# Cluster attention and two MoE layers on one core: probabilities times v over three query tiles at a time instead of two

## The chip, the cores and the metric

The kernel runs on one core of one Trainium2 chip. The metric is the device time of one execution in microseconds; the median of three executions counts. One execution was also profiled, and all rows below are from it. PE is the matrix engine, DVE, ACT and POOL are the three engines for elementwise work, and SP issues the DMAs. PE writes its results to PSUM, in banks of 512 fp32 per partition.

## The reference

```python
q_assign = argmax(q_n @ c_n)      # nearest of 16 centroids, per head; k_assign the same
mask = q_assign[..., :, None] == k_assign[..., None, :]
scores = where(mask, q @ k.T / sqrt(64), -1e9)
attn = exp(scores - max(scores)); attn = attn / (sum(attn) + 1e-9)
x = attn @ v                      # batch 2, 8 heads, 768 tokens, 64 per head -> x [1536, 512]
h = x @ w_in                      # [1536, 1024]
solu = h * softmax(h); ln = layernorm(solu) * g_ln
x = ln @ w_out                    # [1536, 512]
out = ((x @ w_a) * (x @ w_b)) @ w_out2   # inner width 1536
```

Everything is fp32.

## The kernel before

Attention goes over 8 pairs of heads (`n`), two heads `j` in each, six query tiles `t` of 128 rows in each head: 96 steps. A step computes the scores of one query tile against all 768 keys (`score`, PE L989, into one of the two buffers `psS`), their maximum (DVE L993), the exponentials with their sum (ACT L997, into `P_`), and transposes them in two halves of three key tiles (`turn`, PE L1021, into `psT`). The halves are copied to the buffer at `PT_` by DVE (L1028) or ACT (L1030), in turns. `PT_` holds two buffers, one for each group of `GT = 2` query tiles.

After every second step a group is complete, and probabilities times v is run for it (`apply`, PE L1047): six key tiles, each one call to `T.matmul` of 64 columns of v (stationary) against 256 moving columns. Even key tiles go to the left half of the array's columns and so to the upper 64 partitions of `psO`, odd ones to the right half and the lower 64. The six are planned as two pieces (`part` 0 and 1) of three key tiles each, which other PE work may come between. Then ACT copies one half of `psO` (L1061), DVE adds the other (L1062), and, when both heads of the pair are there, the sum of exponentials is inverted (L1067, L1069), spread, transposed (L1077), multiplied in (L1080), and the result is split into a high and a low part for the MoE. In the code there are 8 x 2 x 3 groups, so 96 pieces of three key tiles; the profile has two PE records for each such call.

The two heads of the next pair are prepared between the steps: loads of q, k, v (`do_load`, L658), transposes (`qk_part`, L729), which write the split q and k into a buffer `hl`, similarities to the centroids (`do_sims`: matmul L818, copy to SBUF by ACT L826, transposes L822, reduction L828 into `sim`), the argmax (`do_arg`), one-hots (`ohp`, transposes in `do_oh` and, for the first pair, `do_oh0` L882), and DMAs that place the parts for the score matmuls (`do_place`, L805; `do_ohd`, L911). `hl` has two buffers, used in turns. `do_sims` copies its matmul's result into the buffer of the one-hots.

The first MoE follows, over 12 tiles of 128 tokens (`moe_h` L1140, layer norm, `moe_lnt` L1213, `moe_x2` L1230), then the second (L1283, L1311). Their weights are loaded and split by DVE, ACT and POOL as they are needed; pieces for the second MoE's weights go to 25 places (`PIECES`), three of which are free before the first MoE ends.

The order of all instructions is made at build time by a planner (`Plan`): each operation has an engine, a cost, a rank and what it reads and writes, and a list scheduler sorts them. `ADJ` is a table of additions to the ranks, and `PVC` is the cost that the planner takes for one piece of probabilities times v. Every engine then runs its list strictly in order.

Of the kernel before, what the change touches and what calls it, by code (L numbers as in the profile page):

```python
# [49 lines left out]
    "centroids 0 DVE": 9.936, "centroids 0 PE": 14.146, "centroids 0 POOL": -10.837,  # L50
    "centroids 0 SP": -527.444, "centroids ACT": -19.438, "centroids DVE": 112.978, "centroids PE": -12.208,
    "centroids POOL": -0.395, "centroids SP": 4.39, "direct 0.0 ACT": -59.405, "direct 0.0 DVE": -104.641,
    "direct 0.0 PE": -57.582, "direct 0.1 ACT": -138.753, "direct 0.1 DVE": 1.547, "direct 0.1 PE": -26.219,
    "direct ACT": 76.379, "direct DVE": 60.391, "direct PE": 32.904, "do_arg 0.0.0 DVE": 3.705,
# [11 lines left out]
    "do_load SP": -224.464, "do_oh 1.0 ACT": 1.581, "do_oh 1.0 PE": -8.205, "do_oh 1.1 ACT": 6.451,  # L66
# [23 lines left out]
    "do_sims 5.0 PE": -1.25, "do_sims 5.1 ACT": 7.966, "do_sims 5.1 DVE": 14.282, "do_sims 5.1 PE": 9.306,  # L90
    "do_sims 6.0 ACT": -22.098, "do_sims 6.0 DVE": 71.424, "do_sims 6.0 PE": -51.606,
    "do_sims 6.1 ACT": 45.722, "do_sims 6.1 DVE": -71.608, "do_sims 6.1 PE": -11.805,
    "do_sims 7.0 ACT": 1.712, "do_sims 7.0 DVE": 43.106, "do_sims 7.0 PE": -6.351, "do_sims 7.1 ACT": 0.278,
    "do_sims 7.1 DVE": 1.564, "do_sims 7.1 PE": 17.891, "do_sims ACT": 13.823, "do_sims DVE": -14.384,
    "do_sims PE": -451.772, "gains 0 DVE": 1.737, "gains 0 PE": -123.102, "gains DVE": 10.842,
# [298 lines left out]
def tile_cluster_attention_moe_moe2(  # L394
# [239 lines left out]
    def hlo(n):  # L634
        return HLS[n % 2]
# [759 lines left out]
```

## Time and profile before

| what | us |
|---|---|
| median of 3 executions (751.42 to 752.21) | 751.48 |
| the profiled execution | 752.12 |
| its span from first to last instruction | 750.30 |

A group of instructions of a page or of a view by line is given as line, engine, operation, output <- input, shape and count, then busy time in us, mean ns of one, and idle time of the engine before them with what ended it. The busy time of PE includes an instruction's way through the array, so two that follow each other overlap in the rows; what an instruction costs PE is read here from start to next start in the timeline.

### The profile page before, as it was taken

How to read it: one execution, taken by the hardware profiler on the slowest of the kernel's cores; microseconds unless marked ns; L12 is line 12 of the kernel's file. 1: busy time of each engine (PE TensorE's matmuls, PEld its weight loads, DVE VectorE, ACT ScalarE, POOL GpSimd, SP SyncE). 2: the span in 40 equal slices, each digit the busy share in tenths (PEclk: the TensorE clock that was granted, in tenths of full speed). 3: DMA queues.
4: the chain of work that ended last, by engine and by line, in shares of the span. 5: the costliest groups of instructions: out<-in, count | busy, mean ns of one | idle time of the engine just before them, and what ended most of it. 6: DMA issues, size and time to landing. Idle time of an engine off the chain costs nothing.

```text
span 750.3 us, 11135 instructions
## 1 busy us (share of the span) xinstructions
PE 735.9 (98%) x4152; PEld 590.3 (79%) x4152; DVE 444.6 (59%) x792; ACT 348.6 (46%) x697; POOL 269.4 (36%) x317
## 2 busy tenths in 40 slices
PE   7899999999999999999999999999999999999997
PEld 6667677677777777788998999888888888888886
DVE  5667775867776787699997926882138211112212
ACT  5666676576667666456535544343144211211110
POOL 2116452346264332457461527872047300000000
PEclk8899999999999999999999999999999999999999
DMA  4168545327265211223140222342011000100101
GB/s 149 47 142 206 138 113 130 89 73 156 81 149 126 62 56 41 80 89 113 57 141 2 85 85 94 104 145 80 1 57 56 1 0 1 57 0 1 57 0 57
DMA packets 39093, 58.49 MB, mean 78 GB/s; under 512 B 3832, under 2 KB 33920, under 8 KB 39040
## 3 DMA queue, kind: packets, MB, share of 16 engines
q1 hardware_dynamic: 39040, 57.79, 26.8%
q8 instruction: 33, 0.54, 0.3%
q14 instruction: 20, 0.16, 0.1%
HBM read 36.74 MB, written 3.15 MB: 53 GB/s over the span
## 4 chain that ended last, share of the span: by engine, by line
PE 89%; DVE 5%; DMA 2%; ACT 1%; POOL 1%; issue 1%; SPq 0%; DVEq 0%; ACTq 0%; POOLq 0%
PE psS L1311 13%; PE psT L1283 13%; PE psO L1047 13%; PE psT L1021 9%; PE psS L989 9%; PE psO L1283 7%; PE psM L1283 7%; PE psS L1140 5%; PE psO L1230 4%; PE psM L1230 4%; PE psM L729 1%; PE psM L818 1%; DMA F<-in_moe_w_in_dram 1%; PE psT L1213 1%; DMA F<-in_moe_w_out_dram 1%; PE psM L901 1%
## 5 line engine op out<-in xcount | busy, mean ns | idle before, releaser
L479 POOL TENSOR_TENSOR R<-F,R 128x512 fp32r<-128x512 f32 (+1 forms) x76 | 89.0, 1176 | 73.3 <-ACT R L605 69.5
L1047 PE MATMUL psO<-F 128*64 128x256 f32 x576 | 104.2, 400 | 1.3 <-DVE F L1062 1.3
L1283 PE MATMUL psT<-R 128*128 128x512 f32 x432 | 103.5, 389 | 0.0
L1311 PE MATMUL psS<-R 128*128 128x512 f32 x432 | 103.5, 389 | 0.0
L993 DVE TENSOR_REDUCE mxn<-psS 128x1 f32<-128x768 f32 x96 | 91.3, 952 | 17.8 <-PE psS L989 16.2
L997 ACT ACTIVATE F<-psS,mxn 128x768 f32<-128x768 f32 x96 | 86.8, 904 | 17.7 <-DVE mxn L993 14.4
L1311 PEld LDWEIGHTS psS<-R 128*128 128x128 f32 x432 | 81.0, 188 | 16.8
L1283 PEld LDWEIGHTS psT<-R 128*128 128x128 f32 x432 | 81.0, 188 | 16.8
L989 PE MATMUL psS<-R 128*128 128x512 f32 (+3 forms) x384 | 92.9, 365 | 0.0
L1021 PE MATMUL psT<-ident,F 128*128 128x128 f32 x576 | 90.4, 278 | 0.9 <-ACT F L997 0.4
L1021 PEld LDWEIGHTS psT<-ident,F 128*128 128x128 f32 x576 | 64.8, 140 | 22.7 <-issue 9.2
L989 PEld LDWEIGHTS psS<-R 128*128 128x128 f32 (+1 forms) x384 | 66.5, 193 | 14.5 <-issue 4.6
L596 POOL TENSOR_TENSOR F<-F 128x512 int32<-128x512 int32 x45 | 62.0, 1381 | 38.1 <-DVE F L592 32.6
L1028 DVE COPY F<-psT 128x384 f32<-128x384 f32 x96 | 53.1, 553 | 34.7 <-PE psT L1021 30.9
L1047 PEld LDWEIGHTS psO<-F 128*64 128x64 f32 x576 | 45.7, 137 | 32.9 <-issue 13.4
L1140 PE MATMUL psS<-R 128*128 128x512 f32 x288 | 69.7, 395 | 0.7 <-DVE F L1161 0.7
L1294 ACT COPY F<-psT 128x512 f32<-128x512 f32 x36 | 21.1, 586 | 97.3 <-PE psT L1283 95.7
L1140 PEld LDWEIGHTS psS<-R 128*128 128x128 f32 x288 | 52.8, 188 | 12.7 <-DVE F L1161 1.2
L1030 ACT COPY F<-psT 128x384 f32<-128x384 f32 x96 | 45.9, 478 | 34.5 <-PE psT L1021 32.9
L1296 ACT CAST R<-F 128x512 fp32r<-128x512 f32 x36 | 22.3, 621 | 81.4 <-DVE F L1295 79.9
L1295 DVE TENSOR_TENSOR F<-psO,F 128x512 f32<-128x512 f32 x18 | 12.4, 691 | 73.5 <-PE psO L1283 73.5
L1295 DVE TENSOR_TENSOR F<-psM,F 128x512 f32<-128x512 f32 x18 | 12.4, 690 | 72.5 <-PE psM L1283 72.5
(148 smaller groups left out, 1101.3 us busy)
## 6 DMA issues: line engine op xcount, KB each, us to landing
F<-in_moe_w_out_dram SPq DMA_DIRECT2D x20, 512.0 KB, 3.2
R<-R SPq DMA_DIRECT2D x28, 288.0 KB, 4.6
F<-in_moe_w_a_dram SPq DMA_DIRECT2D x12, 512.0 KB, 3.5
F<-in_moe_w_b_dram SPq DMA_DIRECT2D x12, 512.0 KB, 3.4
R<-R SPq DMA_DIRECT2D x28, 192.0 KB, 4.8
F<-in_moe_w_in_dram SPq DMA_DIRECT2D x8, 512.0 KB, 4.7
F<-in_v_dram SPq DMA_DIRECT2D x8, 384.0 KB, 4.2
out_dram<-F SPq DMA_DIRECT2D x12, 256.0 KB, 2.1
```

The source lines that it names most:

```text
L479: pl.add("POOL", pool(n), rank, lambda: G.tensor_tensor(out=out_, in0=in0, in1=in1, op=ALU.subtract), reads, writes)
L596: pl.add("POOL", pool(n), rank, lambda: G.tensor_tensor(out=u, in0=u, in1=low, op=ALU.add), [rk, lwk], [uk])
L989: T.matmul(sp[:, c0:c0 + cn], kq[:r, 2 * m, t * P:(t + 1) * P], kq[:r, 2 * m + 1, c0:c0 + cn], start=m == 0, stop=m == 1)
L993: pl.add("DVE", dve(S), i + SUB["max"], lambda: V.tensor_reduce(out=mxn[:, b:b + 1], in_=sp[:, :S], axis=AX.X, op=ALU.max, negate=True), [ ...
L997: pl.add("ACT", act(S) + 93 + 93, i + SUB["exp"], lambda: A.activation(F[:, po:po + 768], sp[:, :S], AF.Exp, bias=mxn[:, b:b + 1], scale=1 ...
L1021: T.transpose(sp[:, c, :], pt[:, kt * P:(kt + 1) * P], ident)
L1028: pl.add("DVE", dve(HN), rk, lambda sp=sp, dh=dh: V.tensor_copy(dh, sp), [sk], [hk])
L1047: T.matmul(psO[rs, :GN], vs[:, j, kt % HT * 2 + kt // HT], pt[:, kt, :], start=kt < 2, stop=kt >= NT - 2, tile_position=(0, kt % 2 * D), s ...
L1140: T.matmul(sp[:, n0:n0 + 512], xv5[:, i, a, c], winv[:, w, c, n0:n0 + 512], start=first, stop=(c == KD - 1 and a == 1))
L1230: T.matmul(sp[:, :GN], wo1v(f, w)[:, ds_], d[a][:, f, :], start=(f == 0 and x == 0), stop=(f == NF1 - 1 and x == 2))
L1283: T.matmul(pt, w[:, l, c, :], xv5[:, xs, a, c, :], start=first, stop=(c == KD - 1 and l == 1))
L1311: T.matmul(yv[t][0], hl2[a][:, ts_], wo[:, l, :], start=(first and a == 0 and l == 0), stop=(last and a == 1))
```

## The change

`apply` no longer works on groups of two query tiles in two pieces but on groups of three (`GA = 3`, `AN = 384` columns) in one piece of all six key tiles. `GT = 2` stays for the first MoE. The buffers at `PT_`, the merged result and the spread sums grow from 256 to 384 columns and move within F. There are 32 groups in the place of 48.

R is smaller by 1024 columns: `hl` has one buffer at `HL_`, except that pairs 1 and 3 use a part of the attention's output that isn't written yet. `do_sims` copies into the natural q and k of its own pair (`natv`) instead of the one-hots' buffer, and the second pair has its similarities in a buffer of its own (`simv`). The loads of q and k from pair 3 on have a rank not before the similarities of the pair ahead. The transpose of the gains moves to the start, since its input lies where `PT_` now is. Two instead of three pieces of the second MoE's weights can be loaded before the first MoE's input weights are done with. `PVC` and the table `ADJ` (some 800 numbers) are new.

```diff
-PVC = 3 * 216.0 + 15.0
+PVC = 6 * 324.0 + 260.0
...
-    NG = 3
-    GT = NT // NG
+    GT = 2
     GN = GT * P
+    GA = 3
+    NG = NT // GA
+    AN = GA * P
...
-    KQS, HLS = (20480, 23552, 26624, 36608), (30464, 33536)
-    WO_, EW_, LNT_, HLC_ = 20480, 28672, 31744, 12288 + 6144
-    R = const.tile([P, 39936], F32R, name="R")
+    KQS, HL_ = (20480, 23552, 26624, 33536), 30464
+    WO_, EW_, LNT_, HLC_ = 20480, 28672, 30720, 12288 + 6144
+    R = const.tile([P, 38912], F32R, name="R")
...
+    def simv(n):
+
+        t = natv(1, 1)[:, 1].rearrange("p t d -> p (t d)") if n == 1 else F[:, SIM_:SIM_ + 384]
+        return t.rearrange("p (a h s r c) -> p a h s r c", a=HT, h=2, s=2, r=2)
...
     def hlo(n):
-        return HLS[n % 2]
+        return X0 + 6144 if n in (1, 3) else HL_
...
     def gains():
-        Rk = 6.0
+        Rk = -30.0
...
-        st = F[:, OHP_ + s * HN:OHP_ + (s + 1) * HN]
+        i = (0, 1)[s]
+        st = natv(n, i)[:, 0].rearrange("p t d -> p (t d)")
...
+            if i < 2 and n > 2:
+                rk = max(rk, base(n - 1) + LEAD["sim"] + i * GAP["sim"] + 0.01)
...
     def pto(n, j, g):
-        return PT_ + (n * 6 + j * 3 + g) % 2 * 1536
+        return PT_ + (n * 4 + j * 2 + g) % 2 * 2304
...
-        if part < 2:
-            ks = range(part * HT, (part + 1) * HT)
-
+        if part == 1:
             def mm():
 
-                for kt in ks:
+                for kt in range(NT):
                     rs = slice(kt % 2 * D, (kt % 2 + 1) * D)
-                    T.matmul(psO[rs, :GN], vs[:, j, kt % HT * 2 + kt // HT], pt[:, kt, :], start=kt < 2, stop=kt >= NT - 2,
+                    T.matmul(psO[rs, :AN], vs[:, j, kt % HT * 2 + kt // HT], pt[:, kt, :], start=kt < 2, stop=kt >= NT - 2,
                              tile_position=(0, kt % 2 * D), skip_group_check=True)
 
-            rd = [(o + part * HT * 256, HT * 256), (VS[n % 2] + j * 384, 384)]
-            pl.add("PE", PVC, i + SUB["pv"] + 1 + part, mm, [fc(*rd)], ["psO"], after=70.0)
+            pl.add("PE", PVC, i + SUB["pv"] + 2, mm, [fc((o, NT * AN), (VS[n % 2] + j * 384, 384))], ["psO"], after=70.0)
             return
...
-            pl.add("ACT", act(GN) + 110, rk, lambda: A.copy(xv[hi], psO[lo, :GN]), ["psO"], [hk])
-            pl.add("DVE", dve(GN), rk, lambda: V.tensor_tensor(
-                out=xv[hi], in0=psO[hi, :GN], in1=xv[hi], op=ALU.add), ["psO"], [hk])
+            pl.add("ACT", act(AN) + 110, rk, lambda: A.copy(xv[hi], psO[lo, :AN]), ["psO"], [hk])
+            pl.add("DVE", dve(AN), rk, lambda: V.tensor_tensor(
+                out=xv[hi], in0=psO[hi, :AN], in1=xv[hi], op=ALU.add), ["psO"], [hk])
...
-        if t % GT == GT - 1:
-            task(i + SUB["pv"] + 1, apply, i, 0)
+        if t % GA == GA - 1:
             task(i + SUB["pv"] + 2, apply, i, 1)
...
-    PIECES = [EW_ + i * 1024 for i in range(3)] + [WIN_ + i * 1024 for i in range(6)]
+    PIECES = [EW_ + i * 1024 for i in range(2)] + [WIN_ + i * 1024 for i in range(6)]
```

## Rows read from the trace of the kernel before

**Rows 1.** The page: busy time by engine.
```profile
PE 735.9 (98%) x4152; PEld 590.3 (79%) x4152; DVE 444.6 (59%) x792; ACT 348.6 (46%) x697; POOL 269.4 (36%) x317
```

**Rows 2.** Three stretches: length, then busy time of each engine, granted clock, DMA.
```profile
0.00:40.00 40.00, 32.95 (x183) 25.47 (x184) 23.66 (x52) 24.16 (x51) 7.69 (x33) 0.83 0.36 107
40.00:316.00 276.00, 273.71 (x1763) 197.33 (x1761) 202.76 (x369) 178.52 (x394) 115.35 (x154) 1.00 0.41 106
316.00:440.00 124.00, 123.28 (x794) 111.48 (x793) 108.96 (x237) 66.21 (x115) 67.02 (x66) 1.00 0.28 91
```

**Rows 3.** The page's group of probabilities times v, PE and its weight loads.
```profile
L1047 PE MATMUL psO<-F 128*64 128x256 f32 x576 | 104.2, 400 | 1.3 <-DVE F L1062 1.3
L1047 PEld LDWEIGHTS psO<-F 128*64 128x64 f32 x576 | 45.7, 137 | 32.9 <-issue 13.4
```

**Rows 4.** PE's timeline, 150 to 161 us: start, us, line, shape, count.
```profile
150.43 0.49 PE L1021 MATMUL psT<-ident,F 128*128 128x128 f32 x3
150.85 1.08 PE L1047 MATMUL psO<-F 128*64 128x256 f32 x6
151.86 0.55 PE L1021 MATMUL psT<-ident,F 128*128 128x128 f32 x3
...
156.96 0.55 PE L901 MATMUL psM<-ident,F 128*128 128x128 f32 x3
157.35 0.49 PE L1021 MATMUL psT<-ident,F 128*128 128x128 f32 x3
...
158.40 0.49 PE L901 MATMUL psM<-ident,F 128*128 128x128 f32 x3
158.73 0.49 PE L1021 MATMUL psT<-ident,F 128*128 128x128 f32 x3
```

**Rows 5.** The same timeline where both pieces of a group stand together.
```profile
255.41 1.51 PE L1047 MATMUL psO<-F 128*64 128x256 f32 x12
256.85 0.87 PE L1021 MATMUL psT<-ident,F 128*128 128x128 f32 x6
```

**Rows 6.** The same timeline where the first piece runs.
```profile
34.67 1.97 PE L1047 MATMUL psO<-F 128*64 128x256 f32 x6
36.57 0.90 PE L729 MATMUL psM<-ident,F 128*128 128x128 f32 x3
```

**Rows 7.** The same timeline, 396 to 402 us: matmuls of 256 and of 512 columns.
```profile
396.19 3.04 PE L1230 MATMUL psO<-R 128*128 128x256 f32 x24
399.07 2.91 PE L1140 MATMUL psS<-R 128*128 128x512 f32 x12
401.82 0.38 PE L1213 MATMUL psT<-ident,F 128*128 128x128 f32 x2
```

**Rows 8.** DVE by line and form, 40 to 316 us.
```profile
L1062 DVE TENSOR_TENSOR F<-psO,F 64x256 f32<-64x256 f32 x47 | 19.7, 418 | 7.5 <-ACT F L1061 6.8
```

**Rows 9.** PE's timeline: a piece that waits for the one before it.
```profile
78.52 1.08 PE L1047 MATMUL psO<-F 128*64 128x256 f32 x6 [1.31 <-DVE F L1062]
```

**Rows 10.** PE's timeline: the second pair's first similarities.
```profile
31.92 0.90 PE L822 MATMUL psM<-ident,F 128*128 128x128 f32 x3 [0.57 <-ACT F L826]
```

**Rows 11.** Last placing DMAs of pair 6, and the first transposes of pair 7.
```profile
211.68 2.65 SPq L805 DMA_DIRECT2D R<-R  x3
...
229.65 0.49 PE L729 MATMUL psM<-ident,F 128*128 128x128 f32 x3
```

**Rows 12.** PE's timeline: pair 2's last similarities, pair 3's first transposes.
```profile
66.41 0.49 PE L822 MATMUL psM<-ident,F 128*128 128x128 f32 x3
...
69.11 0.55 PE L729 MATMUL psM<-ident,F 128*128 128x128 f32 x3
```

**Rows 13.** DMA issues by line: a pair's load of q, us to landing last.
```profile
F<-in_q_dram SPq DMA_DIRECT2D x7, 384.0 KB, 3.4
```

**Rows 14.** PE's timeline: last matmuls of w_in, first of the second MoE's w_out2.
```profile
405.94 5.76 PE L1140 MATMUL psS<-R 128*128 128x512 f32 x24
...
465.65 2.68 PE L1311 MATMUL psS<-R 128*128 128x512 f32 x11
```

More of the change, by code (lines that the diff above doesn't have):

```diff
@@ L32 @@
 ADJ = {
[17 rows of a table removed]
[L50 to L54, printed above, removed]
@@ L90 @@
[L90 to L95, printed above, removed]
[43 rows of a table removed]
@@ L210 @@
-    "qk_part 6.1 PE": -1.789, "qk_part 6.1 POOL": 2.238, "qk_part 7.0 ACT": 61.25, "qk_part 7.0 DVE": -5.642,
-    "qk_part 7.0 POOL": 38.884, "qk_part 7.1 ACT": 70.576, "qk_part 7.1 PE": -2.995, "qk_part ACT": -83.604,
-    "qk_part DVE": -105.727, "qk_part PE": -390.481, "qk_part POOL": -509.509, "score 0 ACT": -131.232,
-    "score 0 DVE": 84.395, "score 1 ACT": 71.733, "score 1 DVE": -14.358, "score 1 PE": 0.386,
-    "score 2 ACT": 155.176, "score 2 DVE": -330.202, "score 3 ACT": -13.936, "score 3 DVE": -474.959,
@@ L215 @@
-    "score 3 PE": -0.385, "score 4 ACT": -78.956, "score 4 DVE": -503.533, "score 4 PE": 0.055,
-    "score 5 ACT": -46.042, "score 5 DVE": 35.305, "score 5 PE": -0.129, "score 6 ACT": -48.56,
-    "score 6 DVE": 12.306, "score 6 PE": 0.327, "score 7 ACT": -29.584, "score 7 DVE": -25.409,
-    "score 7 PE": 0.481, "score ACT": 73.266, "score DVE": 65.466, "score PE": -0.383, "setup 0 ACT": 67.137,
-    "setup 0 POOL": 31.423, "setup ACT": -72.736, "setup POOL": -5.235, "turn 0 ACT": -1.436,
-    "turn 0 DVE": -209.322, "turn 1 ACT": -0.328, "turn 1 DVE": 39.126, "turn 2 ACT": 3.373,
@@ new lines @@
+    "centroids 0 SP": 33.608, "centroids ACT": 45.755, "centroids DVE": 8.559, "centroids PE": 12.911,
+    "centroids POOL": 9.375, "centroids SP": -22.931, "direct 0.0 ACT": 53.945, "direct 0.0 DVE": -0.962,
+    "direct 0.0 PE": -4.76, "direct 0.1 ACT": -13.096, "direct 0.1 DVE": 4.166, "direct 0.1 PE": -5.88,
+    "direct ACT": 39.383, "direct DVE": 8.527, "direct PE": -83.71, "do_arg 0.0.0 DVE": -179.162,
+    "do_arg 0.0.1 DVE": 5.621, "do_arg 1.0.0 DVE": 65.445, "do_arg 2.0.0 DVE": -76.294,
@@ new lines @@
+    "do_arg 2.0.0 POOL": 159.228, "do_arg 3.0.0 POOL": -126.55, "do_arg 4.0.0 DVE": 0.683,
+    "do_arg 4.0.0 POOL": -41.278, "do_arg 5.0.0 DVE": -4.248, "do_arg 5.0.0 POOL": -2.925,
+    "do_arg 6.0.0 DVE": -10.118, "do_arg 7.0.0 DVE": -1.388, "do_arg 7.0.0 POOL": 32.387,
+    "do_arg DVE": -644.549, "do_arg POOL": 2.609, "do_load 0.0 SP": -8.215, "do_load 0.1 SP": -0.197,
[5 rows of a table added]
+    "do_load SP": 36.648, "do_oh 1.0 ACT": 1.592, "do_oh 1.0 PE": 10.998, "do_oh 1.1 ACT": 2.15,
[5 rows of a table added]
+    "do_oh 7.0 PE": -11.959, "do_oh 7.1 ACT": 0.028, "do_oh 7.1 PE": 16.032, "do_oh ACT": -44.09,
[10 rows of a table added]
@@ new lines @@
+    "do_sim0 0.1 DVE": -110.869, "do_sim0 DVE": -25.549, "do_sims 1.0 ACT": 0.038, "do_sims 1.0 DVE": -1.813,
+    "do_sims 1.0 PE": -43.843, "do_sims 1.1 ACT": 89.25, "do_sims 1.1 DVE": -42.542,
+    "do_sims 1.1 PE": -43.249, "do_sims 2.0 ACT": -0.446, "do_sims 2.0 PE": -19.798,
+    "do_sims 2.1 ACT": -36.273, "do_sims 2.1 DVE": 4.852, "do_sims 3.0 ACT": 18.798,
+    "do_sims 3.0 DVE": -69.404, "do_sims 3.0 PE": -59.643, "do_sims 3.1 DVE": 1.723,
+    "do_sims 3.1 PE": -18.777, "do_sims 4.0 ACT": -26.908, "do_sims 4.0 DVE": -1.369, "do_sims 4.0 PE": 0.025,
@@ new lines @@
+    "do_sims PE": -279.544, "gains 0 DVE": 37.8, "gains 0 PE": 31.412, "gains DVE": -55.661,
[42 rows of a table added]
+    "load_w2 SP": -5.831, "load_win 0 ACT": 0.217, "load_win 0 DVE": 2.499, "load_win 0 POOL": -54.362,
+    "load_win 0 SP": 9.282, "load_win 1 ACT": -4.481, "load_win 1 DVE": 12.994, "load_win 1 POOL": 447.432,
+    "load_win 1 SP": -181.226, "load_win 2 ACT": 6.192, "load_win 2 POOL": -12.086, "load_win 2 SP": 8.063,
+    "load_win 3 ACT": 58.17, "load_win 3 DVE": 109.45, "load_win 3 POOL": -49.68, "load_win 3 SP": -32.462,
@@ new lines @@
+    "load_win 4 ACT": -26.55, "load_win 4 DVE": 99.889, "load_win 4 POOL": -0.865, "load_win 4 SP": -54.859,
+    "load_win 5 ACT": -1.843, "load_win 5 DVE": -174.107, "load_win 5 POOL": -5.822, "load_win 5 SP": 19.027,
+    "load_win 6 ACT": -30.034, "load_win 6 DVE": -19.496, "load_win 6 POOL": -24.23, "load_win 6 SP": -43.219,
+    "load_win 7 ACT": -35.459, "load_win 7 DVE": -38.916, "load_win 7 POOL": -0.497, "load_win 7 SP": -31.524,
+    "load_win ACT": -23.658, "load_win DVE": 762.513, "load_win POOL": -119.359, "load_win SP": -85.568,
[15 rows of a table added]
@@ new lines @@
+    "moe_ln 0 POOL": 7.043, "moe_ln 1 ACT": 40.837, "moe_ln 1 DVE": 106.067, "moe_ln 1 POOL": 14.368,
+    "moe_ln 10 ACT": 24.689, "moe_ln 10 DVE": 21.796, "moe_ln 10 POOL": -78.923, "moe_ln 11 ACT": 15.885,
+    "moe_ln 11 POOL": -0.232, "moe_ln 2 POOL": 42.434, "moe_ln 3 ACT": 145.42, "moe_ln 3 DVE": 1.79,
+    "moe_ln 3 POOL": 167.863, "moe_ln 4 ACT": -38.788, "moe_ln 4 POOL": 1.208, "moe_ln 5 ACT": -1.043,
+    "moe_ln 5 DVE": -15.008, "moe_ln 5 POOL": -45.958, "moe_ln 6 ACT": -20.861, "moe_ln 6 DVE": 15.816,
@@ new lines @@
+    "moe_ln 6 POOL": -15.299, "moe_ln 7 ACT": -92.533, "moe_ln 7 DVE": 2.327, "moe_ln 7 POOL": 9.643,
+    "moe_ln 8 ACT": -78.612, "moe_ln 8 DVE": -0.982, "moe_ln 8 POOL": 2.655, "moe_ln 9 ACT": 30.566,
+    "moe_ln 9 DVE": 0.758, "moe_ln ACT": 129.305, "moe_ln DVE": 295.975, "moe_ln POOL": 5.335,
+    "moe_lnt 0 ACT": 29.196, "moe_lnt 0 DVE": 36.019, "moe_lnt 0 PE": -38.06, "moe_lnt 1 ACT": -246.407,
+    "moe_lnt 1 DVE": 5.413, "moe_lnt 1 PE": 21.091, "moe_lnt 10 ACT": -3.77, "moe_lnt 10 DVE": 11.428,
@@ new lines @@
+    "moe_lnt 8 DVE": 0.855, "moe_lnt 8 PE": 123.747, "moe_lnt 9 DVE": -70.155, "moe_lnt ACT": 0.648,
[18 rows of a table added]
+    "qk_part 1.1 ACT": -116.128, "qk_part 1.1 PE": -120.406, "qk_part 1.1 POOL": -1.344,
+    "qk_part 2.0 ACT": 49.127, "qk_part 2.0 DVE": -35.088, "qk_part 2.0 POOL": -0.085,
+    "qk_part 2.1 ACT": -17.409, "qk_part 2.1 PE": -38.316, "qk_part 2.1 POOL": 12.816,
+    "qk_part 3.0 ACT": 107.673, "qk_part 3.0 DVE": -15.759, "qk_part 3.0 PE": 14.696,
+    "qk_part 3.1 ACT": 54.432, "qk_part 3.1 PE": -10.271, "qk_part 3.1 POOL": -63.572,
@@ new lines @@
+    "qk_part 4.0 ACT": -149.829, "qk_part 4.0 DVE": -99.679, "qk_part 4.0 PE": 0.708,
+    "qk_part 4.0 POOL": -165.657, "qk_part 4.1 ACT": -2.427, "qk_part 4.1 PE": -17.345,
+    "qk_part 5.0 ACT": 38.684, "qk_part 5.0 DVE": -72.091, "qk_part 5.0 PE": 32.275,
+    "qk_part 5.1 ACT": 35.768, "qk_part 5.1 PE": 1.311, "qk_part 5.1 POOL": 25.114,
+    "qk_part 6.0 ACT": -37.598, "qk_part 6.0 DVE": 0.282, "qk_part 6.0 PE": 1.226, "qk_part 6.0 POOL": -5.031,
+    "qk_part 6.1 ACT": 4.771, "qk_part 6.1 PE": 74.615, "qk_part 7.0 DVE": 25.346, "qk_part 7.0 PE": -76.548,
@@ new lines @@
+    "qk_part 7.1 ACT": 84.626, "qk_part 7.1 PE": 138.929, "qk_part 7.1 POOL": 95.497, "qk_part ACT": -24.163,
+    "qk_part DVE": 0.351, "qk_part PE": -384.816, "qk_part POOL": 289.436, "score 0 ACT": 67.388,
+    "score 0 PE": -70.496, "score 1 ACT": 50.977, "score 1 DVE": -53.625, "score 1 PE": -0.169,
+    "score 2 ACT": 0.028, "score 2 DVE": -58.748, "score 2 PE": -0.447, "score 3 ACT": 15.988,
+    "score 3 DVE": -637.166, "score 3 PE": -0.159, "score 4 ACT": 26.32, "score 4 DVE": -487.991,
@@ new lines @@
+    "score 4 PE": -2.121, "score 5 ACT": 0.59, "score 5 PE": -1.564, "score 6 ACT": -15.462,
+    "score 6 DVE": -60.865, "score 6 PE": -0.246, "score 7 ACT": -0.095, "score 7 DVE": -36.608,
+    "score 7 PE": -0.138, "score ACT": -22.114, "score DVE": 47.0, "score PE": -0.588, "setup 0 ACT": -73.255,
+    "setup 0 POOL": -10.677, "setup ACT": -93.615, "setup POOL": -98.919, "turn 0 ACT": -115.277,
+    "turn 0 DVE": 12.958, "turn 0 PE": -232.204, "turn 1 ACT": 87.305, "turn 1 DVE": 198.807,
+    "turn 1 PE": 0.067, "turn 2 ACT": 6.001, "turn 2 DVE": 13.79, "turn 2 PE": -840.464,
@@ L791, in do_sim0 @@
         pl.add("DVE", dve(NT * 64), rk, lambda: V.tensor_reduce(
-            out=sim[:, :, f, s].rearrange("p a r c -> p r a c"),
-            in_=pv.rearrange("p (r a) g c -> p r a c g", r=2), axis=AX.X, op=ALU.add), [bk], [part("sim", (s,), (f,))])
+            out=simv(n)[:, :, f, s].rearrange("p a r c -> p r a c"),
+            in_=pv.rearrange("p (r a) g c -> p r a c g", r=2), axis=AX.X, op=ALU.add), [bk], [simk(n, (s,), (f,))])
     def do_place(n, j, part, rk):
@@ L1023, in turn @@
             dh = dst[:, hf * HT:(hf + 1) * HT, tt * P:(tt + 1) * P]
-            hk = fc(*[(o + kt * 256 + tt * P, P) for kt in range(hf * HT, (hf + 1) * HT)])
+            hk = fc(*[(o + kt * AN + tt * P, P) for kt in range(hf * HT, (hf + 1) * HT)])
             rk = i + SUB["t1" if hf else "t0"]
@@ L1100, in tile_cluster_attention_moe_moe2 @@
     task(-140, centroids)
-    task(6, gains)
+    task(-30, gains)
     for n in range(NPR):
```

145 lines of the change are left out of this document (54 added, 91 removed), and 225 rows, old and new, of the table ADJ.

## The prediction

> **What bounds the kernel now.** The page comes first: PE is busy 98% of the span, DVE 59%, ACT 46%, POOL 36% [rows 1]. An average over stages proves little, so the view by stretches is next. From 40 to 316 us, where attention runs, PE is busy 273.7 of 276 us at a granted clock of 1.00, the higher of its two levels (2.4 GHz), while DVE has 203 and ACT 179 us of work [rows 2]. From 316 to 440 us, in the first MoE, PE is still busy 123.3 of 124 us, with DVE at 109. Only the first 40 us have gaps: 7 us, at a clock of 0.83. So nearly everything that PE does from 40 us on is on the path that sets the end, and an instruction that goes from PE there is worth its PE time, as long as the others keep up.
>
> The third view is the page's group of probabilities times v: 576 records, 104.2 us busy [rows 3]. The code has 288 calls, so each key tile goes through PE as two passes. Rows of PE overlap, so I go on with PE's timeline, from start to next start.
>
> **What one run costs.** A piece of three key tiles (6 records) takes 150.85 to 151.86, 1.01 us [rows 4]. Once the two pieces of a group stand together, 12 records, and they take 255.41 to 256.85, only 1.44 us [rows 5]. Two separate pieces would take 2.02. The code explains it: even and odd key tiles lie in different column halves of the array and can run at the same time. Three key tiles are a pair and a single one, 2 + 2 = 4 passes one after the other; six are three pairs, 6 passes. With a time s for such a pass and e for the edges of a run, 4s + e = 1.01 and 6s + e = 1.44, so s = 0.215 and e = 0.15 us.
>
> A run costs its neighbours too. Three transposes followed by transposes take 0.33 us (158.40 to 158.73), before a piece 0.42 (150.43 to 150.85), and as the first work behind a piece 0.39 (156.96 to 157.35) [rows 4]. That is 0.09 ahead and up to 0.06 behind. Where scores follow the piece I read less behind it, so I take 0.04, and 0.13 us per run in all.
>
> *Before:* 96 pieces in 95 runs. 94 runs of 1.01 and one of 1.44 make 96.4, and 95 x 0.13 = 12.4 at the neighbours, together 108.8 us. The first piece ran at the lower clock and took 34.67 to 36.57, 0.9 more [rows 6]; I take the start's extra as the same on both sides. As a check, 96.4 plus that, plus 0.07 us of overlap for each of 95 runs, is 104.0, against 104.2 on the page.
>
> *After:* 32 runs of six passes with 384 columns. How a pass grows is read from other matmuls: 24 of 256 columns take 2.88 us, 12 of 512 take 2.75, so 0.120 and 0.229 us each, 1.91 times for twice the columns [rows 7]. From 256 to 384 is half of that step, a factor of 1.455, and gives 0.313; plain proportion gives 0.3225. I take 0.322, since a pass of 0.215 has a smaller fixed share than a matmul of 0.120. A run is 6 x 0.322 + 0.15 = 2.08, with its neighbours 2.21, and 32 of them 70.7 us.
>
> *The difference* is 108.8 - 70.7 = 38.1 us (39.8 with the smaller growth, 29.9 without anything at the neighbours). About 21 us of it is the single key tile's missing partner, 17 us are the 63 runs fewer.
>
> One mechanism would make the difference larger: if a weight load of 0.137 us [rows 3] stood in every pass, that part would not grow with the columns. A pass would be 0.137 + 0.078 x 1.5 = 0.254, a run 1.67, and 32 of them 13 us less than above. Against it: two loads of 0.137 lie in each paired pass of 0.215, so they are hidden. The Trainium skill, "TensorE: Matmul & The Clock Gate", Part 3 (packing small matmuls), says that a load overlaps matmuls in flight only where the row group differs, and here all key tiles use all rows; the trace disagrees by those two loads.
>
> **The other engines.** DVE's adds out of `psO` go from 48 to 32, from 0.418 us [rows 8] to at most 0.63 by proportion, so from 20.1 to 20.2 us at most; the inverse sums and multiplications go down from 24 to 16 likewise, and ACT's copies from 48 to 32. I cost these at nothing: PE's work hides them. If PE falls from 276 to 238 us in this stretch, DVE's 203 us become 85% of it and ACT's 179 become 75%. This cover is thinner, and one run now keeps PE 2.2 us at a stretch while only two score buffers are there to fill DVE and ACT. So I add waits: PE's idle time in the stretch is 2.3 us now [rows 2], and one piece waited 1.31 us [rows 9]; three more such waits make 4 us. Bounds: 0, and 0.5 us at each of 32 runs, 16 us.
>
> **One buffer for `hl`.** The transposes of a pair now wait for the placing DMAs of the pair ahead. ACT and POOL would stand at their writes, with the exponentials queued behind ACT's. The last placing DMAs of pair 6 issue from 211.68 to 214.3, and pair 7's first transposes start at 229.65 [rows 11]. Fifteen us of cover: nothing.
>
> **Loads after the similarities.** q and k of pair n may now load only when pair n-1's similarities have left the natural buffers; in SP's queue the placing DMAs stand behind. It is closest at pair 3: the last similarity transposes of pair 2 at 66.41, its own transposes at 69.11 [rows 12], the load 3.4 us [rows 13]. At worst 66.7 + 3.4 = 70.1, a wait of 1 us, once; I take 0, since the similarities of q end ahead of those of k.
>
> **The one-hots' buffer.** The second pair's copy no longer waits for the first pair's one-hots. PE's own wait for it was 0.57 us [rows 10]; I take 0.5 off, with bounds of 0 and 3 us (more of the start's 7 idle us). The gains' transpose, moved into the start, is one small transpose and one copy: within these bounds.
>
> **Two pieces of weights instead of three.** The third, w_out2's first, now waits for the end of w_in's matmuls, 405.94 + 5.76 = 411.7, and is first used at 465.65 [rows 14]: 54 us for a load and a split of a few us each. Nothing.
>
> **The sum.** 752.12 (the profiled execution) - 38.1 + 4 - 0.5 = 717.5. The median of the runs is 0.64 us under the profiled one, so 717 us.
>
> **The rivals.**
> *B, hand-offs.* PE runs dry after many of the long runs, because the next transposes need an exponential whose scores could not start earlier. At the bound of 0.5 us per run the sum is 12 us worse: 729. For it: DVE at 85%, and blocks twice as long. Against it: from 316 to 440 us DVE is at 88% and PE idles 0.7 us [rows 2].
> *C, slower: `psO` becomes the bound.* There is one `psO`, and a run must wait until ACT's copy and DVE's add have emptied it; if the add stands behind other work in DVE's queue, each of the 32 runs waits. It is slower than before when each waits over (38.1 + 0.5) / 32 = 1.2 us. The one wait of this kind was 1.31 [rows 9]; at every run it is 42 us, and the time 752.1 - 38.6 + 41.9 - 0.6 = 755. Against it: a run comes every 238 / 32 = 7.4 us, and 2.08 for the run, about 0.5 for the copy and 0.6 for the add leave 4 us, and 94 other pieces did not wait.
> The Trainium skill states this as a rule, "TensorEngine Tiling (Array Packing)", Performance Considerations (PSUM Bottleneck): tiling makes PE faster but not the copies out of PSUM, which may become the bottleneck. The trace bears that out in the one wait of rows 9.
> *D, better.* No more waits than now, and the start gains its 3 us: 752.1 - 38.1 - 3 - 0.6 = 710; with the smaller growth of a pass 709.
> *E, the pairs don't hold at 384 columns:* twelve passes in a row, 32 x 6 x 0.322 = 62 us more, 779. Against it: all six passes of 256 columns paired [rows 5], and 384 fit a bank of 512.
> *F, loads that don't grow with the columns:* 704.
>
> **How the numbers follow.** My forecast, 712 to 722, gets 0.56; B, 722 to 733, 0.20; D, 708 to 712, 0.15; C 0.05; E 0.02; F 0.02. The range, 708 to 731, leaves out C, E, F and the end of B. About 0.2% (1.5 us) is what a measurement can tell from no change: faster 0.93 (forecast, B, D and F), same 0.01 (C where its waits just make up for the gain), slower 0.06 (the rest of C, and E).
>
> **What would show it.** In the profile after: 384 records of probabilities times v in runs of 12, each 2.05 to 2.1 us from start to next start, the group some 68 to 70 us busy instead of 104.2; attention done near 280 us; PE's idle time from 40 us to there 4 to 8 us, and DVE near 85%. B would show as PE waiting on the exponentials, of over 10 us in all, C as waits of probabilities times v on the add, E as runs of 4 us. The step that I trust least is the 4 us of waits: the new order of all instructions can't be read from the trace of before, and 800 new ranks can move them either way.

## The result and the profile after

| | before | after |
|---|---|---|
| median, us | 751.45 (4 executions) | 718.42 (717.17 to 721.67, 4 executions) |
| ratio | 1 | 0.9567 (0.9532 to 0.9602) |
| the profiled execution | 752.12 | 717.53 |
| its span | 750.30 | 715.5 |

The forecast was 717.0, 708 to 731. One more set of four executions of the same kernel (`e10_after` below) gave 718.58 (717.68 to 720.29), ratio 0.9556 (0.9533 to 0.9579). The profiled execution is one of the fastest of the eight. It is 34.6 us shorter than the one before, while the medians are 33.0 apart, so some 1.5 us of what the two traces show is luck of the execution.

The page of the kernel after, busy time by engine and the group of probabilities times v, beside [rows 1] and [rows 3]:

```profile
PE 697.1 (97%) x3960; PEld 569.0 (80%) x3960; DVE 437.1 (61%) x752; ACT 345.4 (48%) x679; POOL 264.6 (37%) x295
...
L1048 PE MATMUL psO<-F 128*64 128x384 f32 x384 | 69.0, 494 | 0.0
```

The number after the last bar is PE's idle time ahead of these instructions. It was 1.3 us before and is 0.0 now: not one of the 32 runs waits for `psO`.

The view by stretches (length, then busy time of PE, PEld, DVE, ACT and POOL, granted clock, DMA share, GB/s), beside [rows 2]. The span is 35 us shorter, so the second and third stretch are cut 35 us earlier; attention's last run itself starts at 283.8 us (315.2 before):

```profile
0.00:40.00 40.00, 32.99 (x207) 27.22 (x207) 28.48 (x60) 26.82 (x58) 8.32 (x34) 0.96 0.57 153
40.00:281.00 241.00, 235.90 (x1547) 176.09 (x1548) 192.51 (x326) 173.46 (x374) 112.36 (x136) 1.00 0.45 118
281.00:405.00 124.00, 122.05 (x780) 109.09 (x779) 103.02 (x228) 65.26 (x112) 60.03 (x60) 1.00 0.24 81
```

PE is still the bound. From 40 to 281 us it idles 5.1 us (2.3 before in the longer stretch), DVE is at 80% (the prediction had near 85%) and ACT at 72%.

PE's timeline at about 150 us, beside [rows 4, 5] (start, us, line, shape, count):

```profile
149.84 0.82 PE L1024 MATMUL psT<-ident,F 128*128 128x128 f32 x6
150.58 2.16 PE L1048 MATMUL psO<-F 128*64 128x384 f32 x12
152.67 0.55 PE L823 MATMUL psM<-ident,F 128*128 128x128 f32 x3
```

From 150.58 to 152.67 is 2.09 us. All 32 runs are 12 records, 31 of them take 2.09 us from start to next start and one 2.19.

### The profile page after: what moved, and what is told of

Its sections match the earlier page's. It is cut to its first block, busy times and chain, and to the rows that moved or that the text cites. A ratio compares the mean times of both kernels' runs of the same rounds, so it can differ in the third digit from the quotient of the medians.

```text
span 715.5 us, 10716 instructions
## 1 busy us (share of the span) xinstructions
PE 697.1 (97%) x3960; PEld 569.0 (80%) x3960; DVE 437.1 (61%) x752; ACT 345.4 (48%) x679; POOL 264.6 (37%) x295
## 4 chain that ended last, share of the span: by engine, by line
PE 83%; DVE 6%; ACT 5%; DMA 2%; issue 1%; SPq 1%; POOL 1%; DVEq 0%; ACTq 0%; POOLq 0%
PE psT L1282 14%; PE psS L1310 14%; PE psS L992 7%; PE psT L1024 7%; PE psO L1282 7%; PE psM L1282 7%; PE psO L1048 7%; PE psS L1139 5%; PE psM L1229 5%; PE psO L1229 5%; ACT F L1000 2%; PE psM L819 1%; PE psT L1212 1%; PE psM L729 1%; DVE mxn L996 1%
## 5 line engine op out<-in xcount | busy, mean ns | idle before, releaser
L1024 PE MATMUL psT<-ident,F 128*128 128x128 f32 x576 | 86.1, 276 | 1.8 <-ACT F L1000 1.4
L589 POOL TENSOR_TENSOR F<-F 128x512 int32<-128x512 int32 x45 | 63.8, 1422 | 34.3 <-DVE F L585 19.6
L1296 DVE TENSOR_TENSOR R<-F,R 128x512 fp32r<-128x512 f32 x36 | 32.9, 914 | 64.4 <-ACT R L1295 64.3
L1048 PE MATMUL psO<-F 128*64 128x384 f32 x384 | 69.0, 494 | 0.0
L1031 DVE COPY F<-psT 128x384 f32<-128x384 f32 x96 | 52.7, 549 | 12.3 <-PE psT L1024 11.9
L579 POOL TENSOR_SCALAR F<-F 128x512 int32<-128x512 uint32 x45 | 32.5, 722 | 54.5 <-DMA F<-in_moe_w_b_dram 12.3
L1282 PE MATMUL psO<-R 128*128 128x512 f32 x216 | 51.9, 389 | 0.0
```

Of the source, the lines that this page charges most:

```text
L589: pl.add("POOL", pool(n), rank, lambda: G.tensor_tensor(out=u, in0=u, in1=low, op=ALU.add), [rk, lwk], [uk])
L1024: T.transpose(sp[:, c, :], pt[:, kt * P:(kt + 1) * P], ident)
L1031: pl.add("DVE", dve(HN), rk, lambda sp=sp, dh=dh: V.tensor_copy(dh, sp), [sk], [hk])
L1048: T.matmul(psO[rs, :AN], vs[:, j, kt % HT * 2 + kt // HT], pt[:, kt, :], start=kt < 2, stop=kt >= NT - 2, tile_position=(0, kt % 2 * D), s ...
L1282: T.matmul(pt, w[:, l, c, :], xv5[:, xs, a, c, :], start=first, stop=(c == KD - 1 and l == 1))
```

## The experiments

Theory 1 is the prediction's: six key tiles are six paired passes, 0.322 us each at 384 columns, and each run costs edges; the rest of PE's work stays what it was. What speaks against it would be a gain that comes from elsewhere: from the new order, from the freed buffers, or from the third query tile alone. Each label below is one kernel.

### Two and three pieces in the place of one

The changed kernel in its own order, but each run is cut, and PE's next operation goes between the pieces; once into two pieces of three key tiles, once into three of two. What is left of a run is issued at the latest before the first operation of any engine that needs its result.

```diff
+                first, *rest = [(0, 1, 2), (3, 4, 5)]
...
-                for kt in range(NT):
+                for kt in ks:
```

In the second kernel the list is `[(0, 1), (2, 3), (4, 5)]`.

> The changed kernel with its own order, except that each run of six key tiles is cut into two of three, with the next PE operation between them. Theory 1: 2 x (4 x 0.322 + 0.15) = 2.88 instead of 2.08 us in each of 32 groups, 25.5 us more, and 32 more runs at 0.13 for the neighbours, 4 us: 718.4 + 30 = 748 (744 to 752). Rival (the new order and fewer operations for each pair carry the gain, not the pairs): below 735.

> The changed kernel with its own order, except that each run of six key tiles is cut into three of two, each with the next PE operation behind it, so that every key tile keeps its partner. Theory 1: 64 more runs at 0.15 + 0.13 = 0.28 us, 18 us more: 736 (732 to 741), so less than with two pieces of three. Rival (each interruption costs, and the lone third key tile does not): as much again as with two pieces of three, twice its cost, 750 or more.

The two pieces: 750.55 us (749.20 to 751.46), ratio 0.9979 (0.9969 to 0.9989), so nearly the whole gain is lost with 384 columns, 32 groups and all buffers unchanged. The three pieces: 741.66 (741.26 to 742.26), just above the expected range. Timelines of PE, first with two pieces, then with three:

```profile
150.91 1.50 PE L1063 MATMUL psO<-F 128*64 128x384 f32 x6
152.35 0.97 PE L1007 MATMUL psS<-R 128*128 128x512 f32 x4
```

```profile
160.43 0.87 PE L1063 MATMUL psO<-F 128*64 128x384 f32 x4
161.22 0.55 PE L838 MATMUL psM<-ident,F 128*128 128x128 f32 x3
161.70 1.51 PE L1063 MATMUL psO<-F 128*64 128x384 f32 x8
163.14 0.98 PE L1007 MATMUL psS<-R 128*128 128x512 f32 x4
```

The second kernel is not quite what was meant. In 27 of its 32 groups an operation that needs the result came so early that the last two pieces ran together, as here: two key tiles, other work, then four. Only five groups ran as three pieces of two, so there are 69 runs and not 96. What a pass takes can be read from it all the same: a piece of three tiles (6 records) takes 1.44 us, one of two (4 records) 0.80, and one of four (8 records) 1.44, the same as three. With s = 0.322 and e = 0.15 the sum gives 4s + e = 1.44, 2s + e = 0.79 and again 4s + e = 1.44. So the lone third tile costs as much as a pair, and 69 runs without lone tiles cost less than 64 with them (741.66 and 750.55 us). The time of the second kernel does not fit the terms as well: 37 more runs at 0.28 us would be 10.4 us, 729, and 13 more were measured. Of these 8.7 are idle time of PE from 40 us to its last run (13.8 us, 5.1 in the changed kernel); the rest stays open.

### One piece, still 256 columns

First the kernel before in its own order, with the two pieces of a group issued together, at the later one's place or the last that the data allow:

```diff
+            for p0, p1 in at.get(k, ()):
+                self.ops[p0][3]()
+                self.ops[p1][3]()
```

> The kernel before with its own order of instructions, except that the two pieces of a group of two query tiles are put together, one run of all six key tiles with 256 columns at the place of the second piece (earlier where its buffer is needed). Theory 1 (PE's time goes with the paired passes and the number of runs): 48 runs of 1.44 instead of 95 of 1.01 take 27 us out, and 47 runs fewer at 0.13 us for the neighbours 6 us more: 751.5 - 33 = 718, or up to 726 with new waits, since this order was not made for long runs. Rival (the gain needs three query tiles or the new order of all instructions): 740 or more.

738.86 us (737.57 to 741.13), ratio 0.9822 (0.9803 to 0.9842): outside theory 1's 718 to 726, and by its number nearer to the rival. Its group in the page and one run:

```profile
L1062 PE MATMUL psO<-F 128*64 128x256 f32 x576 | 74.7, 396 | 0.0
...
153.25 1.52 PE L1062 MATMUL psO<-F 128*64 128x256 f32 x12
154.69 0.55 PE L916 MATMUL psM<-ident,F 128*128 128x128 f32 x3
```

The runs do what theory 1 said: 1.44 us each, and the group's busy time falls by 29.5 us against [rows 3]. What is missing from the expected 33 us is for the most part waits. The order was made for short pieces, and counted over all gaps between PE's starts, as what each has above the median of its kind, attention has 20.6 us of them in the place of 2.8. PE's idle time alone, as the profile has it from 40 us to the last run, is 12.1 us in the place of 2.3.

So the same was tried with an order that fits. This kernel has the changed kernel's buffers, groups of two tiles (`GA = 2`, `AN = 256`, 48 runs), and ranks searched anew with the same planner (`PVC` and the views of `PT_` follow):

```diff
-    GA = 3
+    GA = 2
```

> The changed kernel's buffers, but groups of two query tiles: 48 runs of six key tiles with 256 moving columns, and an order of all instructions fitted to that by the same planner. Theory 1 (the terms of the sum: the partner of the lone key tile, and then the number of runs): 48 x (1.44 + 0.13) = 75.4 us against 32 x (2.08 + 0.13) = 70.7, so 4.7 us more than the changed kernel plus 0 to 5 us of waits: 723 to 728. Rival 1: the third query tile is what brings the gain (longer runs, fewer adds and waits), and merging alone leaves most of the loss: 735 or more, as the merged run with an order that was not made for it (738.9). Rival 2: pairing alone brings everything: 720 or less.

727.71 us (727.27 to 731.94), ratio 0.9686 (0.9661 to 0.9711): inside theory 1's 723 to 728, though near its end, and both rivals fall. Of the 33 us, 24 come with one piece in the place of two, a fitted order and the new buffers together, and 9 more with the third query tile: 4.7 by the terms. The rest goes with waits and a lower granted clock in this order (0.84 from 40 to 80 us, 1.00 from there to 281), but the profile is of the slowest of its five executions, so this part is not shown. Nor are these shares of single causes: cutting the runs costs 32 us in the changed kernel, and taking back two buffers, below, 11, which is more than 33 together. A kernel with the new buffers, a fitted order and two pieces of two query tiles was not run.

```profile
154.64 1.52 PE L1549 MATMUL psO<-F 128*64 128x256 f32 x12
156.09 0.55 PE L1230 MATMUL psM<-ident,F 128*128 128x128 f32 x3
```

### The one-hots' buffer again

The changed kernel with the similarities back in the one-hots' buffer, and the second pair without one of its own:

```diff
-        t = natv(1, 1)[:, 1].rearrange("p t d -> p (t d)") if n == 1 else F[:, SIM_:SIM_ + 384]
+        t = F[:, SIM_:SIM_ + 384]
...
-        i = (0, 1)[s]
-        st = natv(n, i)[:, 0].rearrange("p t d -> p (t d)")
+        st = F[:, OHP_ + s * HN:OHP_ + (s + 1) * HN]
```

Three orders were tried: the same ranks, the changed kernel's own order as far as the data allow, and ranks searched anew.

> The changed kernel with the similarities copied into the one-hots' buffer again and the second pair's similarities in the common buffer, the order made anew with the same ranks. Theory 1 (the freed buffer is worth 0.5 us at the start, 3 at most): 719 to 722, the difference inside the first 60 us. Rival (the freed buffer carries a good part of the gain): 725 or more.

> The similarities go through the one-hots' buffer and the common buffer again, as in the run before this, but the instructions keep the changed kernel's order wherever these buffers allow it, instead of an order made anew. Theory 1 (the freed buffers are worth little by themselves; what the earlier run lost, 37 us, was its unfitted order): 719 to 723. Rival (the second pair's preparation can't run ahead without the freed buffers, and that is most of the 37 us): 735 or more.

> The changed kernel, but with the similarities in the one-hots' buffer again as before the change, and an order of all instructions fitted to that by the same planner. Theory: in a kernel of 32 long runs the common buffer holds up the second pair's preparation and costs several us whatever the order, 723 to 731 us. Rival: the 11 us that the common buffer cost in the order of the changed kernel were only those of an order not made for it, and a fitted one needs no more than 720 us (my 0.5 us, bound 3).

They gave 755.20 us (750.16 to 757.66), 729.21 (728.53 to 730.06) and 743.55 (740.69 to 746.25). Every number lies above what I expected; the first fits its rival, the second lies between its two theories and the last above both. Where the time goes is best seen with the second of them, which differs least. The first run of probabilities times v, first in the changed kernel, then here:

```profile
35.12 2.16 PE L1048 MATMUL psO<-F 128*64 128x384 f32 x12
```

```profile
40.24 0.90 PE L967 MATMUL psM<-ident,F 128*128 128x128 f32 x3 [0.57 <-ACT F L971]
...
45.03 3.98 PE L1192 MATMUL psO<-F 128*64 128x384 f32 x12
```

Counting the scores (48 records a pair) gives the start of the second pair: 54.2 us in the changed kernel, 65.8 here, 11.6 later. Every later pair and the end are as much behind, between 11.5 and 11.9 us. So in the changed kernel's order the two own buffers are worth 11 us, not my 0.5, nor my bound of 3. Part of it is the clock: from 30 to 50 us the granted clock was 0.76 and 0.56 here, 1.00 there, and the run shown takes 1.8 us longer by it. In the searched order the second pair starts at 64.0; that order then loses another 13 us between the fifth and the eighth pair, where the same buffers cost the kernel in the changed order nothing, so its total says little on the buffers. The kernel before started the second pair at 56.3 with the common buffers. How early a 32-run kernel with them could start at best stays open.

### Matmuls to fill the start's waits

The changed kernel, with 31 transposes whose result nobody reads, put into five of the start's waits:

```diff
+    FILLERS = {26: ("psO", 6), 34: ("psM", 7), 43: ("psT1", 3), 58: ("psO", 7), 66: ("psM", 8)}
...
+        for _ in range(n):
+            T.transpose(bank[bk][:, :P], ident, ident)
```

> The changed kernel with 31 more transposes of the identity, whose results nobody reads, put into five of PE's waits in the first 33 us. Theory (executions of the changed kernel differ, 717.2 us at a mean granted clock of 0.997 and 721.7 at 0.989, because the clock falls to its lower level behind PE's waits at the start): 714 to 717 us, all executions within 1 us, granted clock 0.997 or more. Rival (the clock falls whatever PE does there, or the executions differ for another reason): 717 to 722 as without them.

720.18 us (719.77 to 720.67), ratio 0.9578 (0.9565 to 0.9592): not faster, as the rival said. The granted clock (0.998 to 0.999) and the spread came as the theory had them, the time did not. The stretch from 10 to 20 us, here and then in the changed kernel, has a granted clock of 1.00 in the place of 0.83:

```profile
10.00:20.00 10.00, 7.71 (x56) 6.07 (x56) 6.69 (x14) 6.40 (x14) 2.01 (x3) 1.00 0.20 57
```

```profile
10.00:20.00 10.00, 7.76 (x45) 5.92 (x45) 6.86 (x14) 6.89 (x15) 2.44 (x4) 0.83 0.20 60
```

The clock was held, and yet the third pair starts at 87.5 us, in the changed kernel at 87.6. Nothing had been won before that either: in the first 40 us PE got through 237 instructions, 206 without the 31 that were put in, and through 207 in the changed kernel, and the second pair starts at 54.7 us, in the changed kernel's two profiles at 54.2 and 55.0. So the lower clock from 10 to 20 us did not set the pace of the start; what does was not taken apart. The next experiments look at what stands between the second pair and the third.

### The wait for pair 3's k

The longest new wait of PE in attention is for pair 3's k. The changed kernel, PE's timeline, then SP's queue:

```profile
62.80 0.49 PE L1024 MATMUL psT<-ident,F 128*128 128x128 f32 x3
64.90 0.52 PE L729 MATMUL psM<-ident,F 128*128 128x128 f32 x3 [1.61 <-DMA F<-in_k_dram]
...
68.82 0.55 PE L729 MATMUL psM<-ident,F 128*128 128x128 f32 x3 [0.63 <-DVE F L1080]
```

```profile
52.74 5.09 SPq L805 DMA_DIRECT2D R<-R  x6
57.93 0.54 SPq L658 DMA_DIRECT2D F<-in_k_dram  x1
```

The load goes to the natural buffer of k, of which there is one, and pair 2's similarities now lie there. It was free by 55.4 us, when pair 2's last similarity transposes (L823, 54.94) were done. The load stood behind six placing DMAs until 57.93, and it landed 7 us later. The edit issues it as soon as all that it depends on has been issued, ahead of the last two of them:

```diff
+        need = set(self.ops[ld[0]][4])
...
+            if need:
+                need.discard(i)
+                if not need:
+                    self.ops[ld[0]][3]()
```

> The changed kernel once more, unchanged, beside the three others of this group. Its four times so far lie between 717.2 and 721.7 us, and go with the granted clock of the whole execution (0.997 to 0.989). Expected 717 to 719 where the clock is 0.996 or more, and up to 722 where it is lower; the ratio to the kernel before 0.955 to 0.960.

> The changed kernel with one SP instruction moved: the load of pair 3's k is issued as soon as pair 2's k similarities have left the natural buffer, ahead of the last two of the six placing DMAs that stood before it. Theory: the 1.61 us that PE waited for it at 64.90 us is a stall of the single buffer and of SP's queue, and PE is the bound behind it; the wait is gone (under 0.3 us left) and the time falls by 1.2 to 1.6 us, to 716 to 717.5. Rival: work behind the wait is held by something else too, the microsecond is given back by the next pair, and the time is that of the changed kernel within 0.5 us.

The changed kernel gave 718.58 us, this one 720.62 (719.12 to 722.12). The load went out at 56.44 us and the wait for it was gone, as the theory said; the time was not shorter. It is 2.0 us longer, more than the rival's 0.5, but the intervals of the ratios overlap (0.9581, 0.9558 to 0.9603). PE and DVE in this kernel:

```profile
67.33 0.49 PE L1034 MATMUL psT<-ident,F 128*128 128x128 f32 x3
70.65 0.90 PE L739 MATMUL psM<-ident,F 128*128 128x128 f32 x3 [2.82 <-DVE F L1090]
```

```profile
68.83 0.43 DVE L582 TENSOR_SCALAR F<-F 128x512 f32<-128x512 f32 x1 [3.25 <-DMA F<-in_moe_w_in_dram]
69.18 0.95 DVE L1006 TENSOR_REDUCE mxn<-psS 128x1 f32<-128x768 f32 x1
70.05 0.55 DVE L1090 TENSOR_TENSOR F<-F,psM 128x384 f32<-128x384 f32 x1
```

Here is the real holder: DVE's first split of the second w_in piece stands at the head of DVE's queue until that piece has landed. A maximum and the multiplication out of `psM` are queued behind it, and PE waits for the multiplication. The three waits are one thing seen from different sides. In the changed kernel's first profile 1.61 + 0.63 = 2.24 us, in its second 0.29 + 1.96 = 2.25: what PE doesn't wait for k it waits for DVE. Part of it is chance of the loads: k took 7.0 us to land in the first profile and at most 5.9 in the second. And the split began at 67.01 and 67.99 us in these two profiles, at 68.83 with the load of k moved and at 66.97 in the kernel with the filled start, each time just when its piece had landed, 6.4 to 7.9 us behind its issue:

```profile
66.97 0.43 DVE L579 TENSOR_SCALAR F<-F 128x512 f32<-128x512 f32 x1 [1.70 <-DMA F<-in_moe_w_in_dram]
```

So this one piece of weights, needed 200 us later, holds the work there. The last two kernels move DVE's first split of that piece behind the five instructions that were queued after it, once alone and once together with the load of k:

```diff
+        order.remove(win[0])
+        order.insert(order.index(win[1]), win[0])
```

> The changed kernel with one DVE instruction moved: the first split of the second w_in piece, which held DVE for 2.3 us until that piece's DMA had landed (67.0 us), now stands behind the five maxima, copies and the multiplication that were queued after it, just ahead of its own successor. Reading: two waits lie one behind the other near 65 us, PE's for pair 3's k load (0.3 to 1.6 us) and DVE's for the w_in piece, which comes to PE as a wait on the multiplication (0.6 to 2.0 us); together they are 2.2 us in each profile. Expected: the second is gone, the first stays, 716.5 to 718. Moving the load of k alone gave nothing because the second then grew to 2.8 us. Rival: the waits come back behind them as others and the time stays within 0.5 us of the changed kernel's 718.6.

> Both instructions moved: pair 3's load of k ahead of the last two placing DMAs, and DVE's first split of the second w_in piece behind the five instructions queued after it. Expected by the same reading: no wait over 0.5 us between 60 and 72 us, the granted clock of 40 to 80 us at 1.00, and 715 to 716.5, 2 to 3 us under the changed kernel on the same chip and with a smaller spread, since the clock was seen to fall just behind a wait of 2 us. Rival: within 0.5 us of the changed kernel.

They gave 716.75 us (715.90 to 718.05), ratio 0.9537 (0.9516 to 0.9558), and 717.64 (716.72 to 717.86), ratio 0.9543 (0.9524 to 0.9561). PE's timeline with the split alone moved, the same place:

```profile
67.82 0.49 PE L1028 MATMUL psT<-ident,F 128*128 128x128 f32 x3
68.15 0.49 PE L733 MATMUL psM<-ident,F 128*128 128x128 f32 x3
68.47 0.52 PE L1028 MATMUL psT<-ident,F 128*128 128x128 f32 x3
```

The wait on the multiplication is gone in both, and none above 0.2 us is left between 62 and 72 us. With the split alone moved I had expected the wait for k to stay; it did not, since the load had landed by 64.8 us, at most 5.9 behind its issue. In this stretch the reading holds: from the second pair's first scores to the third pair's it is 33.4 and 35.1 us in the changed kernel's two profiles, 37.2 with the load of k alone, 31.5 and 32.0 in the last two. Of these 2 to 3 us, 1 to 2 reach the medians. The intervals of the ratios overlap those of the changed kernel, so I can't call either of the two shown to be faster; the second missed its 715 to 716.5. Moving k as well brought nothing beside the split.

## Why the prediction held, point by point

The bookkeeping is PE's, start to next start, summed over the two profiled traces: 34.8 us less, where the prediction's sum has 34.6. By its terms:

- **In the runs.** Predicted 97.3 (with the start's 0.9) to 66.6 us plus some extra, 29.9 less; the traces have 97.60 to 66.87, 30.7 less, and the start's extra is gone. The growth of a pass by 1.455 (0.313 us) would have made a run 2.03; plain proportion, which I took, gave 2.08, and 2.09 was measured. The split experiments then reproduced s and e at 384 columns.
- **At the neighbours.** Predicted 8.2 less. What is left of the difference when runs and waits are taken out is about 6, most of it at the transposes of `turn` (3.4) and of q and k (1.9). By this count the 0.13 us per run was somewhat too much. The count depends on which gaps are taken as of one kind: outside the runs the traces differ by 4.1 us, and how these are shared between neighbours, waits and the start moves by 1 to 3 us with it.
- **Waits in attention.** Predicted +4 (0 to 16). What PE's gaps have above the median of their kind went from 2.8 to 7.4 us, +4.6. The size was right, but not the kind: I priced them as waits for `psO`, and there is none. By PE's idle time, 2.3 us before and 5.1 now, it is +2.8. The largest waits are the chain at 65 us, of two loads and DVE's queue. That the size came out is luck.
- **Loads after the similarities.** I took 0, at worst 1.0 us at pair 3. This was the right place, and a mis-sized term: 1.61 us in one profile, 0.29 in the other. I priced the load at the 3.4 us of [rows 13], which is the median of q's loads (k's is 5.2 in the same view), and let it start as soon as the buffer was free; it stood 2.5 us behind the placing DMAs and took 7 us to land. I had named that queue and not costed it.
- **The one-hots' buffer and the start.** Predicted -0.5 (0 to -3). Gaps of the first 45 us fell by 3.9, from 11.5 to 7.5, and the second pair starts 2.1 us earlier. Part of it is the granted clock of these two executions, as the rows at the end show, and the two own buffers as such are worth 11 us in this order. This is the term that was mis-sized most. The bound was worked out from one wait in an order made for the common buffer, and didn't see what the new order needs.
- **The first MoE.** Predicted 0; its gaps rose from 1.2 to 2.4 us, most of it one wait of 2.0 us at 300.7 us.
- **DVE's adds.** 0.63 us was the bound by proportion, 0.553 us is measured (by line and form, 40 to 281 us), and PE hides them as predicted:

```profile
L1062 DVE TENSOR_TENSOR F<-psO,F 64x384 f32<-64x384 f32 x30 | 16.6, 553 | 9.1 <-ACT F L1061 8.6
```

Attention's last run starts at 283.8 us, not near 280. Matmuls of the first MoE come between its last ones from 265.5 us on, as they did before the change.

By this count the errors nearly cancel: 2 us too much at the neighbours, 2 too few in waits, 3 too few at the start. So the sum is closer to the measured time than its terms are, and that is luck.

Of the rivals, B would have shown over 10 us of waits on the exponentials; they are 2.1 in the whole span (waiting engine and line, what it waits for, us in all, times, longest):

```profile
PE psT L1024 <- ACT F L1000: 1.4, 4, 0.5
...
PE psS L992 <- ACT F L1000: 0.7, 1, 0.7
```

Of D the gain at the start came, the rest did not, since waits rose. C and E are excluded by the 0.0 us ahead of the runs and by their 2.09 us. The Trainium skill's rule for C ("TensorEngine Tiling (Array Packing)", PSUM Bottleneck) is not borne out by this trace: copies out of `psO` are a bottleneck nowhere. The mechanism by which a run would have been 1.67 us, for which I had set the Trainium skill's "TensorE: Matmul & The Clock Gate", Part 3 (packing small matmuls), against the trace, is excluded by the 2.09 too: the pass grew with its columns.

## What to carry to other kernels

Where a run is cut, count the passes, not the matmuls: with two column halves, an odd number of tiles leaves one pass half empty, and here three tiles took as long as four. Judge a regrouping only in an order made for it; the same merged runs were worth 13 us in the old order, and 24 in a fitted one with the new buffers. And follow a wait to the head of the queue that holds it, since a wait that an engine shows may only stand in front of another one: removing the wait for k alone gained nothing.

## What the runs showed of the hardware

The granted clock of the start is not the same in all profiles, and PE's pace goes with it. The first 40 us, in steps of 10, second and fourth step of the profile before, then the fourth of the profile after:

```profile
10.00:20.00 10.00, 7.69 (x39) 5.59 (x37) 6.63 (x13) 6.61 (x15) 1.52 (x2) 0.66 0.21 65
...
30.00:40.00 10.00, 8.60 (x35) 5.48 (x36) 3.70 (x7) 4.34 (x10) 1.50 (x2) 0.66 0.28 70
```

```profile
30.00:40.00 10.00, 8.42 (x56) 5.68 (x54) 7.98 (x14) 7.28 (x18) 0.65 (x1) 1.00 0.83 183
```

Between 30 and 40 us PE got through 35 instructions at 0.66 and through 56 of much the same kind at 1.00. The time of the whole need not: the kernel with the filled start had a granted clock of 1.00 in all of the first 40 us (0.96 in the changed kernel) and 0.998 to 0.999 over the span, and took 719.77 to 720.67 us. The eight executions of the changed kernel lie between 717.17 us (granted clock 0.997 over the whole span) and 721.67 (0.989), but two with 0.995 took 717.75 and 720.29.

In some cases a single long wait of PE was followed by a fall of the clock, and so cost more than itself. From 70 to 80 us, behind the waits at 65 to 70 us, the granted clock was 1.00 in the changed kernel's first profile (waits of 1.61 and 0.63 us), 0.83 in its second (0.29 and 1.96), 0.66 with the load of k moved (2.82) and 1.00 with the split moved (none above 0.2). In this order:

```profile
70.00:80.00 10.00, 10.00 (x71) 8.09 (x70) 8.62 (x15) 8.08 (x18) 5.18 (x5) 1.00 0.61 158
```

```profile
70.00:80.00 10.00, 10.00 (x59) 7.78 (x59) 6.79 (x12) 7.02 (x17) 5.64 (x6) 0.83 0.47 112
```

```profile
70.00:80.00 10.00, 9.35 (x44) 6.93 (x45) 6.76 (x12) 6.17 (x13) 5.29 (x7) 0.66 0.43 104
```

```profile
70.00:80.00 10.00, 9.95 (x70) 7.56 (x70) 9.12 (x16) 7.90 (x19) 5.52 (x7) 1.00 0.59 146
```

In the changed kernel's two profiles the waits of this stretch add up to the same, and with the clock at 0.83 behind them it took 35.1 us in the place of 33.4. This goes together in four profiles, but the length of the wait is not all: at another place, in the first MoE, PE waits 1.95 us in the changed kernel and the granted clock stays at 1.00, while in the kernel with the filled start it waits 1.85 us and the clock is 0.83 there. Each wait and its stretch, in this order:

```profile
300.70 1.65 PE L1139 MATMUL psS<-R 128*128 128x512 f32 x6 [1.95 <-DVE F L1160]
...
300.00:310.00 10.00, 9.29 (x45) 7.70 (x46) 10.00 (x28) 6.51 (x12) 5.27 (x6) 1.00 0.23 89
```

```profile
301.61 1.22 PE L1146 MATMUL psS<-R 128*128 128x512 f32 x4 [1.85 <-DVE F L1167]
...
300.00:310.00 10.00, 8.39 (x32) 6.80 (x33) 9.05 (x19) 5.64 (x10) 5.07 (x5) 0.83 0.18 56
```

What else the clock depends on wasn't varied.
